# Additions behind the out product of batches 0 and 1, made by adding transfers instead of by VectorE

## The chip, the cores and the metric

The kernel runs on one core of one Trainium2 chip. A core has a matrix engine (TensorE; PE in the profile, with its weight loads as PEld), VectorE (DVE), ScalarE (ACT), GpSimd (POOL) and a queue engine, SyncE (SP). Each takes its own instructions strictly in order and waits on semaphores for the others. DMA transfers are issued by SP, by POOL and, in four places at the end, by ACT. The metric is the device time of one execution in microseconds (us); less is better.

## The reference, cut to what matters

All data are float32. B is 8, H is 8, S is 576, D is 64, and C is H x D, 512.

```python
kv  = einsum('bhsd,bhse->bhde', k, v)                 # attention without softmax
out = einsum('bhsd,bhde->bhse', q, kv)
x   = out / sqrt(mean(out*out, -1) + 1e-6) * g_norm   # then (B, S, H*D)

gate = sigmoid(causal_conv(x, conv_w))                # 5 taps along the sequence, per channel
val  = x @ w_val
y    = (gate * val) @ w_out                           # (B, S, 512)
```

## The kernel before, in words

**Order.** No scheduler chooses the order. A long string, `PLAN`, lists 1235 steps, each a function name with small integers, and the main loop calls them in that order. What a step issues stands behind what earlier steps issued on the same engine. Stores and loads go to the SP queue, in the order of their steps. A tile framework adds the semaphore waits, from the tiles and DRAM regions that an instruction reads and writes.

**Stages of a batch b.** `load_half` and `load_q` bring k, v and q; `kv_product` and `kv_copy` make kv; `turn_q` transposes q on VectorE; `raw_pair b c` makes the attention product of chunks c and c-1 (128 tokens each) in two PSUM banks, `raw_tail` that of the last 64 tokens. `square` (ACT) and `sums` (DVE) give the sums of squares; `powers` (POOL, L552) turns them into reciprocal roots; `normalise` (ACT, L571) scales with them and so frees the PSUM banks of the raw product. `turn_blocks` (DVE, L596) transposes 32x32 blocks into `y`, and `move_blocks b a` (L604) moves `y` into the channel-major tile `xT` with four transfers, two from SP and two from POOL. The last 64 tokens go another way: `turn_x b 4` transposes them on TensorE, and `keep_x` evicts them. `halo` (POOL, L611) fills the four tokens that the convolution looks back to. Then `gate_start`, four times `gate_tap`, `gate_end`, and beside them `x_sums` (DVE, L667) and `val_fast` (PE, L682) for x @ w_val. `gated` leaves gate * val in `gv`.

**The out product.** Two batches make a pair i (i = 0 is batches 0 and 1). A pair has four blocks p of 256 tokens, each with two chunks c = 2p and c = 2p+1 of 128 tokens, and a chunk 8 for the tails of both batches (`out_product`, `keep_out`). The blocks are multiplied by a seven-product scheme: `fast_product i p n`, n = 0 to 6, adds into three half banks, a (one PSUM bank) and b, c (halves of another, named cb). `fast_keep i p n` takes results out when they are due:

- n = 0 and n = 2 (ACT copies, L786 and L790) put a into the low and the high half of the first chunk's tile `ot`; n = 1 (ACT, L788) puts c into the high half of the second chunk's tile; n = 6 (ACT, L797) puts a into its low half.
- n = 5 (DVE, L784 by a helper) adds the whole bank cb, 512 columns, to the first chunk; n = 4 (DVE, same line) adds a, 256 columns, to the high half of the second chunk.

`store i c` (L806) then writes a chunk with four SP transfers of 32 rows of 2 KB.

For pair 0 the plan runs `fast_product` from 73.65 us on, beside batch 1's gates and batches 2 to 4's earlier stages. The string around the second and third store (nothing left out between `store 0 1` and `powers 3 0`):

```
store 0 1; load_q 4 1; store 0 3; gate_tap 1 2 1;
normalise 3 1; halo 2; powers 3 0; ... store 0 2; ... normalise 3 0; fast_keep 0 2 0; turn_blocks 3 0
```

and around its last one:

```
move_blocks 4 2; store 0 7; move_blocks 4 0; kv_copy 5 0; move_blocks 4 1; ... move_blocks 4 3;
... powers 4 4; normalise 4 4; ... turn_x 4 4; ... val_fast 4 0 0
```

Of the kernel before, what the change touches and what calls it, by code (L numbers as in the profile page):

```python
# [9 lines left out]
FP32 = mybir.dt.float32  # L10
U32 = mybir.dt.uint32
AF = mybir.ActivationFunctionType
ALU = mybir.AluOpType
AX = mybir.AxisListType

P = 128
# [191 lines left out]
def kernel(  # L208
# [11 lines left out]
    nc = tc.nc  # L220
    B, H, S, D = q.shape
    C = H * D
    HP = H // 2
    NJ = S // P
# [8 lines left out]
    HB = P // TB  # L233
# [7 lines left out]
    FAST_OUT = 0  # L241
    ROOTS = {(0, 2): H + H // 2, (0, 1): 2 * H}
    GATES = 3
    GVS = 3
    assert NJ == 4 and NB == 18
    assert 2 * T == P and NB * TB == S and SV <= 512 and C <= 512 and D == 2 * TB
# [3 lines left out]
    work = ctx.enter_context(tc.tile_pool(name="work", bufs=2))  # L250
# [9 lines left out]
    xTs = [const.tile([P, NK, SX], FP32, name=f"xT{i}") for i in range(2)]  # L260
    gv = const.tile([P, NK, GVS * S], FP32, name="gv")

# [13 lines left out]
    LOW, HIGH = slice(0, C // 2), slice(C // 2, C)  # L276
# [19 lines left out]
    st = {}  # L296
# [100 lines left out]
    for jt in range(NK):  # L397
        cols = slice(jt * P, (jt + 1) * P)
# [214 lines left out]
    def gate_start(b, jt):  # L613
        gate = work.tile([P, S], FP32, tag="gate", bufs=GATES, name=f"gate{b}_{jt}")
        nc.scalar.activation(  # L615
            out=gate[:], in_=xTs[b % 2][:, jt, HALO:SX], func=AF.Copy, scale=cwT[:, K - 1, jt:jt + 1])
        st["gate", b, jt] = gate
# [22 lines left out]
    def keep_val(b, jt, n):  # L640
        first = b % GVS * S + n * SV
        nc.scalar.copy(out=gv[:, jt, first:first + SV], in_=st["val", b, jt, n][:])

    def gated(b, jt):
        both = gv[:, jt, b % GVS * S:(b % GVS + 1) * S]
        nc.vector.tensor_tensor(out=both, in0=both, in1=st["gate", b, jt][:], op=ALU.mult)  # L646
# [39 lines left out]
    def val_keep(b, mj, n):  # L686
        a, b_, c = (st[bank, "val", b, mj][:] if (bank, "val", b, mj) in st else None for bank in "abc")
        to = lambda o, half: gv[:, mj + 2 * o, b % GVS * S + half * SV:b % GVS * S + (half + 1) * SV]
        add = lambda out, one, two: nc.vector.tensor_tensor(out=out, in0=one, in1=two, op=ALU.add)
# [15 lines left out]
    rows_out = out.rearrange("b (t n) c -> b n t c", n=NB)  # L705

    def out_product(i, c):

        po = ps([P, C], f"out{i}_{c}")
        for jt in range(NK):  # L710
            if c < 2 * NJ:
                first = (2 * i + c // NJ) % GVS * S + c % NJ * P
                nc.tensor.matmul(
# [4 lines left out]
            for r in range(2):  # L718
                first = (2 * i + r) % GVS * S + SF
                nc.tensor.matmul(  # L720
# [57 lines left out]
    def fast_keep(i, p, n):  # L778
        a, b, c = (st.get((bank, i, p)) for bank in "abc")
        row = int(n in (1, 4, 6))  # L780
        if ("ot", i, 2 * p + row) not in st:
            st["ot", i, 2 * p + row] = work.tile([P, C], FP32, tag="ot", bufs=3, name=f"ot{i}_{2 * p + row}")
        first, second = (st.get(("ot", i, 2 * p + r)) for r in range(2))
        add = lambda out, one: nc.vector.tensor_tensor(out=out, in0=one, in1=out, op=ALU.add)  # L784
        if n == 0:
            nc.scalar.copy(out=first[:, LOW], in_=a)  # L786
        elif n == 1:
            nc.scalar.copy(out=second[:, HIGH], in_=c)  # L788
        elif n == 2:
            nc.scalar.copy(out=first[:, HIGH], in_=a)  # L790
        elif n == 4:
            add(second[:, HIGH], a)
        elif n == 5:
            add(first[:], st["bc", i, p][:].rearrange("p r c -> p (r c)"))
        else:
            last = (i, p) == (B // 2 - 1, 2 * NV - 1)
            (nc.vector.tensor_copy if last else nc.scalar.copy)(out=second[:, LOW], in_=a)  # L797

    def store_last(i, c, n):
        store(i, c, nc.scalar if n else nc.sync, range(n * HB // 2, (n + 1) * HB // 2))  # L800

    def store(i, c, queue=nc.sync, blocks=range(HB)):
        ot = st["ot", i, c]
        for j in blocks:
            bb, n = divmod(c * HB + j, NJ * HB) if c < 2 * NJ else (j // 2, NJ * HB + j % 2)
            queue.dma_start(out=rows_out[2 * i + bb, n], in_=ot[j * TB:(j + 1) * TB, :])  # L806

    steps = {f.__name__: f for f in (
        load_half, load_q, load_q_rows, stage_weight, narrow_weight, turn_cw, keep_cw, start_warm, warm_up,
        kv_product, kv_copy, turn_q, turn_q_rows, sort_q, raw_whole, raw_pair, raw_tail, square, sums, powers, normalise,  # L810
        turn_x, keep_x, turn_blocks, move_blocks, halo, gate_start, gate_tap, gate_end, val_product, keep_val, gated,
        val_sums, x_sums, val_fast, val_keep, out_product, keep_out, weight_sums, token_sums, fast_product, fast_keep,
        store, store_last)}
    with tc.manual_schedule():
        set_up()
# [33 lines left out]
```

## Time and profile before

| | |
|---|---|
| time, two runs | 305.83 and 306.24 us, median 306.03 |
| span of the profiled execution | 304.6 us |
| TensorE busy, matmuls (modelled ends) | 294.8 us, 97% |
| VectorE busy | 269.2 us, 88% |
| ScalarE busy | 193.7 us, 64% |
| GpSimd busy | 114.9 us, 38% |
| HBM read, written | 39.21 MB, 9.44 MB |

The profile was taken of one execution, and its span runs from the first to the last instruction. A whole execution's time is some 1.4 us more than this span (306.03 against 304.6). A row of a timeline gives start and duration in us, engine, line, operation and tiles, then how long the engine sat idle before it and which engine ended that. The chain of work that ended last is followed back from the last instruction, at each step to what released it.

### The profile page before, as it was taken

How to read it: one execution, taken by the hardware profiler on the slowest of the kernel's cores; microseconds unless marked ns; L12 is line 12 of the kernel's file. 1: busy time of each engine (PE TensorE's matmuls, PEld its weight loads, DVE VectorE, ACT ScalarE, POOL GpSimd, SP SyncE). 2: the span in 40 equal slices, each digit the busy share in tenths (PEclk: the TensorE clock that was granted, in tenths of full speed). 3: DMA queues.
4: the chain of work that ended last, by engine and by line, in shares of the span. 5: the costliest groups of instructions: out<-in, count | busy, mean ns of one | idle time of the engine just before them, and what ended most of it. 6: DMA issues, size and time to landing. Idle time of an engine off the chain costs nothing.

```text
span 304.6 us, 8977 instructions
## 1 busy us (share of the span) xinstructions
PE 294.8 (97%) x3441; PEld 232.4 (76%) x3441; DVE 269.2 (88%) x474; ACT 193.7 (64%) x596; POOL 114.9 (38%) x127
## 2 busy tenths in 40 slices
PE   7899999999999999999999999999999999999993
PEld 7788778877787785777778757787878588888582
DVE  1169999999999999999999999999999999999612
ACT  1569989999768664884586547683787354535220
POOL 3027354406568217364338352345536631000000
PEclk9979999999999999999999999999999999999999
DMA  7999998088569756988689477927411621112423
GB/s 269 343 368 343 272 302 210 4 230 269 154 147 329 231 163 167 269 220 260 173 253 294 111 175 232 326 72 214 114 48 30 169 80 34 36 42 64 103 69 103
DMA packets 32074, 55.53 MB, mean 182 GB/s; under 512 B 6166, under 2 KB 14358, under 8 KB 32032
## 3 DMA queue, kind: packets, MB, share of 16 engines
q1 hardware_dynamic: 29520, 49.76, 55.7%
q0 software_dynamic: 1632, 3.17, 4.1%
q10 hardware_dynamic: 880, 2.03, 1.8%
q8 instruction: 27, 0.44, 0.6%
q14 instruction: 15, 0.12, 0.1%
HBM read 39.21 MB, written 9.44 MB: 160 GB/s over the span
## 4 chain that ended last, share of the span: by engine, by line
PE 89%; DVE 5%; DMA 2%; issue 1%; ACT 1%; DVEq 0%; ACTq 0%; SPq 0%
PE a L774 18%; PE cb L774 14%; PE va L682 13%; PE val L633 11%; PE vc L682 6%; PE kvps L440 6%; PE raw L501 5%; PE out L720 5%; PE vb L682 4%; PE qTps L477 4%; PE raw L512 2%; PE xTps L583 2%; DMA qs<-in_q_dram 2%; DVE gate L621 2%; DVE xs L667 1%
## 5 line engine op out<-in xcount | busy, mean ns | idle before, releaser
L552 POOL TENSOR_TENSOR rt<-ss,mhalf 128x8 f32<-128x8 f32 (+3 forms) x38 | 68.9, 1822 | 101.0 <-DVE ss L544 100.8
L621 DVE SCALAR_TENSOR_TENSOR gate<-xT,cwT,gate 128x576 f32<-128x576 f32 x128 | 101.8, 809 | 1.0
L571 ACT ACTIVATE x<-raw,rt 128x64 f32<-128x64 f32 x252 | 55.8, 351 | 7.2 <-POOL rt L552 4.2
L604 POOL DMA_DIRECT2D xT<-y x48 | 26.4, 557 | 25.5 <-DVE ot L784 14.0
L633 PE MATMUL val<-xT,wval 128*128 128x288 f32 x128 | 33.0, 411 | 0.0
L774 PE MATMUL a<-wsum,sums 128*128 128x256 f32 x128 | 32.4, 382 | 0.0
L628 ACT ACTIVATE gate<-gate 128x576 f32<-128x576 f32 x32 | 22.0, 692 | 11.7 <-DVE gate L621 11.4
L633 PEld LDWEIGHTS val<-xT,wval 128*128 128x128 f32 x128 | 23.5, 190 | 6.5 <-ACT xT L590 0.4
L544 DVE TENSOR_REDUCE ss<-sq 128x8 f32<-128x520 f32 (+1 forms) x40 | 24.7, 627 | 2.9 <-ACT sq L531 2.5
L774 PEld LDWEIGHTS a<-wsum,sums 128*128 128x128 f32 x128 | 24.0, 190 | 4.1 <-issue 0.6
L535 ACT ACTIVATE sq<-raw 128x256 f32<-128x256 f32 (+1 forms) x70 | 22.4, 403 | 7.3 <-PE raw L501 7.1
L682 PE MATMUL va<-xs,vsum 128*128 128x288 f32 x96 | 26.6, 409 | 0.0
L615 ACT ACTIVATE gate<-xT,cwT 128x576 f32<-128x576 f32 x32 | 25.2, 811 | 1.5 <-DVE gv L646 1.3
L646 DVE TENSOR_TENSOR gv<-gv,gate 128x576 f32<-128x576 f32 x32 | 23.6, 750 | 0.9 <-ACT gate L628 0.8
L682 PEld LDWEIGHTS va<-xs,vsum 128*128 128x128 f32 x96 | 18.0, 190 | 5.1 <-ACT x L571 0.4
L611 POOL COPY xT<-xT 128x124 f32<-128x124 f32 x32 | 17.5, 585 | 10.5 <-ACT xT L590 10.5
L501 PEld LDWEIGHTS raw<-kv,qT 64*64 64x64 f32 x1008 | 16.4, 134 | 5.3 <-issue 3.0
L440 PEld LDWEIGHTS kvps<-v,k 64*64 64x64 f32 x1008 | 15.9, 135 | 3.7 <-issue 1.9
L501 PE MATMUL raw<-kv,qT 64*64 64x64 f32 x1008 | 18.7, 221 | 0.0
L440 PE MATMUL kvps<-v,k 64*64 64x64 f32 x1008 | 17.6, 220 | 0.0
L774 PE MATMUL cb<-wsum,sums 128*128 128x256 f32 x64 | 16.9, 386 | 0.1
L774 PE MATMUL cb<-wout,gv 128*128 128x256 f32 x64 | 16.8, 385 | 0.0
(111 smaller groups left out, 542.3 us busy)
## 6 DMA issues: line engine op xcount, KB each, us to landing
qs<-in_q_dram SPq DMA_DIRECT2D x96, 140.0 KB, 4.2
out_dram<-ot SPq DMA_DIRECT2D x140, 64.0 KB, 1.7
k<-in_k_dram SPq DMA_DIRECT2D x14, 576.0 KB, 6.3
v<-in_v_dram SPq DMA_DIRECT2D x12, 576.0 KB, 6.5
xT<-y SPq DMA_DIRECT2D x48, 64.0 KB, 2.7
xT<-y POOLq DMA_DIRECT2D x48, 64.0 KB, 3.3
y<-in_moe_w_val_dram SPq DMA_DIRECT2D x4, 512.0 KB, 11.4
w_wout<-in_moe_w_out_dram SPq DMA_DIRECT2D x4, 512.0 KB, 6.3
```

Source lines behind the costliest of these rows:

```text
L440: nc.tensor.matmul(st["kvps", b][s][r * D:(r + 1) * D, i], st["k", b, i][rows, r, cols], st["v", b, i][rows, r, cols], start=(j == 0), sto ...
L501: nc.tensor.matmul(st["raw", b, c][r][cols, to * D:(to + 1) * D], st["qT", b][rows, hp, first:first + D], kvs[b % 2][rows, hp, :], start=T ...
L544: nc.vector.reduce_sum(out=st["ss", b][:, FIRST[c]:FIRST[c] + n], in_=st["sq", b, c][:, 0:n], axis=AX.X)
L552: nc.gpsimd.tensor_tensor(out=st["rt", b][:, which], in0=st["ss", b][:, which], in1=mhalf[:, which], op=ALU.pow)
L571: nc.scalar.activation(out=x[:, to * D:(to + 1) * D], in_=raw[:, h * D:(h + 1) * D], func=AF.Copy, scale=root[:, to:to + 1])
L604: (nc.sync if i % 2 else nc.gpsimd).dma_start(out=xTs[b % 2][i * TB:(i + 1) * TB, :, first:first + P], in_=y[a * TB:(a + 1) * TB, i])
L615: nc.scalar.activation(out=gate[:], in_=xTs[b % 2][:, jt, HALO:SX], func=AF.Copy, scale=cwT[:, K - 1, jt:jt + 1])
L621: nc.vector.scalar_tensor_tensor(out=gate[:], in0=xTs[b % 2][:, jt, tap * TB:tap * TB + S], scalar=cwT[:, tap, jt:jt + 1], in1=gate[:], op ...
L633: nc.tensor.matmul(val[:], wval[:, kc, jt * P:(jt + 1) * P], xTs[b % 2][:, kc, HALO + n * SV:HALO + (n + 1) * SV], start=(kc == 0), stop=( ...
L646: nc.vector.tensor_tensor(out=both, in0=both, in1=st["gate", b, jt][:], op=ALU.mult)
L682: nc.tensor.matmul(st[bank, "val", b, mj][:], weights_[:, k], tokens()[:, k], start=(n in (0, 1, 3) and k == 0), stop=(k == NK // 2 - 1), ...
L774: nc.tensor.matmul(st[bank, i, p], tokens()[:, k], weights_[:, k], start=(n < 2 and k == 0), stop=(k == NK // 2 - 1), skip_group_check=True)
```

## The change

A tuple `ADDED_OUT = (0,)` names the pairs concerned: pair 0, that is batches 0 and 1, 8 of the 32 additions of L784. For these, `fast_keep` with n = 4 or 5 no longer adds with VectorE. ScalarE copies the PSUM half or bank into a new SBUF tile, `more4` (256 columns, two buffers) or `more5` (512 columns, one buffer). The chunk's plain store writes the incomplete sum; behind it, in the same step, POOL issues one transfer that adds `more` to these rows of the output (`accum_op=ALU.add`). The plan string is the same.

```diff
+    ADDED_OUT = (0,)
...
+        elif n in (4, 5) and i in ADDED_OUT:
+            part, cols = (a, HIGH) if n == 4 else (st["bc", i, p][:].rearrange("p r c -> p (r c)"), slice(0, C))
+            more = work.tile([P, C if n == 5 else C // 2], FP32, tag=f"more{n}", bufs=6 - n, name=f"more{i}_{p}_{n}")
+            nc.scalar.copy(out=more[:], in_=part)
+            st["more", i, 2 * p + row] = more, cols
         elif n == 4:
             add(second[:, HIGH], a)
         elif n == 5:
...
             queue.dma_start(out=rows_out[2 * i + bb, n], in_=ot[j * TB:(j + 1) * TB, :])
+        if ("more", i, c) in st:
+            more, cols = st["more", i, c]
+            bb, n = divmod(c * HB, NJ * HB)
+            nc.gpsimd.dma_start(
+                out=rows_out[2 * i + bb, n:n + HB, :, cols], in_=more[:], accum_op=ALU.add)
```

In the built program each adding transfer waits for five or six semaphores: those of the four plain stores of its chunk, and those of its own earlier transfer slot and of the ScalarE copy where these are not already known to be past. On the POOL queue the eight of them stand as follows (named by the step that issues them):

```
powers 2 4
ADD store 0 0
move_blocks 2 0, 2 2, 2 1, 2 3     (8 transfers; the last one reuses the semaphore of ADD store 0 0)
powers 3 3, 3 2, 3 1
ADD store 0 1
ADD store 0 3
halo 2
powers 3 0
ADD store 0 2
move_blocks 3 1, powers 3 4, move_blocks 3 3, 3 2, 3 0
ADD store 0 4
powers 4 3
ADD store 0 5
powers 4 2
ADD store 0 6
powers 4 1, 4 0
halo 3
move_blocks 4 2
ADD store 0 7
move_blocks 4 0, 4 1, 4 3
powers 4 4
```

The other engines keep their order, but for the eight additions that leave VectorE and the eight copies that join ScalarE.

## The prediction

> **What bounds the kernel now.** I read the busy times and the chain first:
>
> ```profile
> PE 294.8 (97%) x3441; PEld 232.4 (76%) x3441; DVE 269.2 (88%) x474; ACT 193.7 (64%) x596; POOL 114.9 (38%) x127
> ...
> PE 89%; DVE 5%; DMA 2%; issue 1%; ACT 1%; DVEq 0%; ACTq 0%; SPq 0%
> ```
>
> TensorE holds 89% of the chain, VectorE 5%. PE's busy time is modelled, so I asked for stretches of 10 us around the change (columns: busy us of PE, PEld, DVE, ACT and POOL with counts, granted clock, DMA share, GB/s):
>
> ```profile
> 90.00:100.00 10.00, 10.00 (x44) 8.01 (x43) 9.86 (x15) 8.55 (x30) 8.76 (x8) 1.00 0.94 300
> 100.00:110.00 10.00, 9.66 (x190) 7.79 (x189) 9.96 (x19) 6.97 (x27) 0.62 (x1) 1.00 0.74 209
> ```
>
> Both PE and VectorE are full. That PE really streams shows in the chain: four 288-column matmuls take 0.97 us at their fastest, and 44 matmuls in 10 us is that rate. So an easier VectorE gives little, and a stall of TensorE is not made up later. One place in this stretch is tight, in the chain's pieces (start, length):
>
> ```profile
> 106.44 0.27 ACT x L571
> ...
> 106.85 1.34 ACT x L571 x6
> 108.20 0.04 issue
> 108.24 2.16 PE a L774 x8
> ```
>
> This is `normalise 3 0`: when its last piece ends, PE gets a bank and goes on 0.04 us later. From 89.9 to 106.4 the chain stands on VectorE. What feeds `normalise 3 0` besides is `powers 3 0` on POOL (timeline of POOL):
>
> ```profile
> 92.60 3.71 POOL L552 TENSOR_TENSOR rt<-ss,mhalf 128x8 f32<-128x8 f32 x2 [0.94 <-DVE ss L544]
> 96.27 1.97 POOL L611 COPY xT<-xT 128x124 f32<-128x124 f32 x4
> 98.54 2.08 POOL L552 TENSOR_TENSOR rt<-ss,mhalf 128x8 f32<-128x8 f32 x1 [0.30 <-DVE ss L544]
> 113.09 1.16 POOL L604 DMA_DIRECT2D xT<-y  x2 [12.47 <-DVE ot L784]
> ```
>
> It ends at 100.6, 5.8 us ahead of need. And the stores of the changed chunks (timeline of SP; L320 is `load_q 4 1`, the row of eight is `store 0 3` and `store 0 2`):
>
> ```profile
> 94.04 2.07 SPq L806 DMA_DIRECT2D out_dram<-ot  x4
> 96.80 4.60 SPq L320 DMA_DIRECT2D qs<-in_q_dram  x4
> 101.51 4.34 SPq L806 DMA_DIRECT2D out_dram<-ot  x8
> ```
>
> **Part 1, eight additions leave VectorE.** From the groups by form, 4 of 680 ns and 4 of 408 ns, 4.35 us busy; by the starts of their neighbours they hold 0.60 and about 0.31 us each, 3.6 us of queue time. Worth: only the one at 91.23 lies in the VectorE piece of the chain, 0.6 us at most. Before and after it TensorE streams anyway.
>
> **Part 2, eight copies join ScalarE.** By its copies of PSUM: 128x512 takes 600 ns (L728), 128x256 some 390 ns (L786), so 4 x 0.60 + 4 x 0.39 = 4.0 us on an engine 64% busy. One of them waits: the copy of n = 5 of block 1 needs products that PE ends at 91.02, and behind it stand the squares of batch 3, which ran from 89.9 to 91.28. They now end near 92.9, so `sums 3 2` starts at 92.9, not at 91.83: VectorE's piece is 1.1 us later, and `normalise 3 0` could start at 107.5, not 106.44. At 79 the same pattern (copy behind 79.72, `normalise 2 0` 1.05 us later) is used up by 83.97, where ScalarE sat idle for 1.29 us. Part 1's gain is gone with this; part 3 covers the rest.
>
> **Part 3, eight adding transfers join POOL.** Each waits there for its chunk's stores to land, with the roots and halos queued behind it. Issue: the nearest rows are POOL's own transfers, 557 ns (L604) and 610 ns (L406); I take 0.6. I bound it by 0.5 and, for twice the rows of such a transfer, 1.2.
>
> - `ADD store 0 0`: its plain store no longer waits for VectorE (SP waited 5.8 us for that, until 80.71), so it lands near 82. Nothing urgent is behind it but transfers that start at 82.7. No cost.
> - `ADD store 0 1` and `ADD store 0 3`, **the main cost**. The stores of chunk 1, issued from 94.04, landed after 6.5 to 7.2 us, behind four loads of 576 KB (DMA share 0.94): about 101.5. Those of chunk 3 leave SP from 101.51 on, the last at about 103.1, and took 1.9 us more: 105.0, with part 2's shift upstream 105.3. Only then POOL goes on: 0.6 issue, halo 1.97, powers 2.08 (109.95), and `normalise 3 0` starts at 110.0. From its start to PE's next matmul it took 108.24 - 106.44 = 1.8, so PE goes on at 111.8: **+3.6 us**, with part 2's 1.1 inside it. VectorE loses 2.7 there (its next step waits for the same `normalise`), so it gains 0.9 on PE and does not bound next.
> - `ADD store 0 4`, `0 5`, `0 6` between the roots of batch 4. Their stores need no addition any more and come up to 1.2 us sooner; counted on the old clock they land at 120.3, 122.9 and 130.1. So `powers 4 3` ends at 123.0 and `powers 4 2` at 125.7, against needs at 123.86 and 125.72. No cost, 0 to 1 us.
> - `ADD store 0 7`, **the second cost**. Now POOL issues all eight `move_blocks` of batch 4 and the last root in one run, while SP's half is slower:
>
> ```profile
> 141.35 4.39 POOL L604 DMA_DIRECT2D xT<-y  x8 [4.17 <-issue]
> 145.75 1.04 POOL L552 TENSOR_TENSOR rt<-ss,mhalf 128x4 f32<-128x4 f32 x1
> ```
>
> The stores of chunk 7 leave SP from 143.46 to 145.2 and landed after 3.6 to 4.3 us: 149.4, or 148.5 if fewer POOL transfers run beside them, which I take. Then 0.6 issue, six transfers of 0.55, the root 1.04: 153.4, not 146.8. `normalise 4 4` (0.93) ends at 154.4; PE's `turn_x 4 4` stood at 151.89: +2.6. The transfers for `val_fast 4 0 0`, right behind, land in the same time (151.3 + 3.3 to 4.3). ScalarE has 3.2 us of work backed up behind `normalise 4 4`, so `normalise 5 2` comes 4.0 late, 1.4 more than PE; I take 0.4 of it. **+3.0 us**, bounds 1.6 and 4.4.
>
> Moved bytes: 1.5 MB in, and as much read back, on 55.5 MB; most of it outside the full stretch at 90 to 100. Nothing.
>
> **Who waits for an adding transfer to land?** The last transfer of `move_blocks 2 3` (same semaphore), and the copy into `more5` (one buffer). No row shows such a transfer. From below: 64 KB by POOL lands in 3.3 us (transfers xT<-y); from above: a 576 KB load under the full load took 7.8 us. I take 5, nearer the plain loads' 4.1 to 6. The slacks are then enough: issued at 82, wanted by 89; issued at 110.5, its buffer wanted at 120; issued near 125, wanted near 133. So no cost at 5, and none up to 7.
>
> [...]
>
> **Sum.** 0 + 3.6 + 0 + 3.0 = 6.6 us on a span of 304.6: 311.2. With the 1.4 us around it (306.03 - 304.6), 312.6 us; waits priced at nothing above (0 to 1 us each) add more often than they take, so I say **313.0**. Of this kernel about 2%, 6.1 us, can be told from no change, which is 312.15: the forecast lies close to that.
>
> **The rivals.**
>
> - *Forecast: the roots wait on POOL behind the stores.* 310 to 316: 306.0 and the two costs at their low ends (2.6, if chunk 3's stores run 1 us sooner, and 1.6) or at their high ones (3.6 and 4.4, and 1.8 more for three issues of 1.2). Chance 0.58.
> - *The waits are absorbed.* If PE has other banks to go on with, and chunk 3's and 7's stores land 2 us sooner, 306 to 310. For: 5.8 us of spare at `powers 3 0`. Against: 105.0 is 4.4 us past its old end, 100.6. Chance 0.16.
> - *The adding transfers land late.* [...] Past 7 us the last move of batch 2 and with it `x_sums 2 0` (92.46) slip one for one, of which the fixed stall at 108 hides 3.6; past 9 the copies into `more5` hold ScalarE. With 10 us that is 0 and 1 on top of 313, 314; with 14, 3.4 and 5, 321. For: many such transfers follow each other with one buffer. Against: the output's 64 KB stores land in 1.7. Chance 0.22. [...]
> - *Other side: VectorE was the true bound.* If the 269.2 us of VectorE set the end in this stretch, and the modelled PE only looks full, 3.6 us of queue time come off: 306.0 - 3.6 = 302.4. It decides only if POOL is ready before VectorE reaches 105.7, that is if chunk 3's stores land by 100.5. Against: they were issued at 101.5. Chance 0.04.
>
> **Numbers.** Slower by over 2% (above 312.15): six tenths of the forecast's chance (0.35) and all of the third rival (0.22), 0.57. Within 2%: the rest, 0.42; the other side's 302.4 is within it too. Faster by over 2% (below 299.9) would need more than all eight additions are worth: 0.01. The likeliest case alone spans 310 to 316; for 8 in 10 I take 307.5 to 320, which cuts the low end of the second rival and the high end of the third.
>
> **What would show it.** Right: in the waits, POOL's halo or root waiting for a DMA of the output; `normalise 3 0` starting near 110, PE idle some 3 us ahead of block 3's first product; a second gap of PE ahead of `turn_x 4 4`, with the last root of batch 4 some 6 us later than its neighbours. VectorE's additions 24, ScalarE's busy time up by 4 us. Wrong: PE's gaps the same as before and POOL's waits harmless; or ScalarE waiting for the output's transfers (third rival); or store 0 3 leaving SP before 99.

## The result, and the profile after

The changed kernel takes 329.35 us (328.80 and 329.89), against 306.03 before: a ratio of 1.077, 95% interval 1.071 to 1.084. It is slower by 23 us, where 6.6 were forecast. Its profiled execution has a span of 327.0 us, against 304.6.

Busy times and the shares of the chain that ended last, from the page of the changed kernel (a line of the code has a number one higher than before, behind the new branch six higher; L816 is the adding transfer, L795 the copy into `more`):

```profile
PE 300.6 (92%) x3441; PEld 234.3 (72%) x3441; DVE 267.1 (82%) x466; ACT 196.6 (60%) x604; POOL 123.6 (38%) x135
...
PE 63%; DMA 18%; DVE 4%; SPq 4%; POOL 3%; ACT 2%; issue 2%; ACTq 0%; POOLq 0%; DVEq 0%
```

TensorE held 89% of the chain; now it has 63%, and transfers, which had 2%, have 18%. The stretches of 10 us, with the columns as in the prediction:

```profile
90.00:100.00 10.00, 7.08 (x23) 5.48 (x24) 6.92 (x10) 5.07 (x19) 5.83 (x4) 0.83 0.99 297
100.00:110.00 10.00, 10.00 (x99) 7.83 (x101) 8.17 (x16) 7.03 (x24) 3.73 (x6) 1.00 0.72 179
...
140.00:150.00 10.00, 7.12 (x20) 5.31 (x21) 5.36 (x8) 6.11 (x19) 6.02 (x7) 0.66 0.57 130
...
170.00:180.00 10.00, 8.51 (x82) 5.96 (x81) 7.00 (x12) 6.88 (x27) 3.15 (x2) 0.59 0.84 246
```

At 90 to 100, 23 matmuls stand where 44 stood before. And the granted clock, 1.00 in these stretches before, is 0.83, 0.66 and 0.59 in three of them. So time went in two ways, waits and a slow clock. The waits are these rows of TensorE's timeline, all of those between 86 and 180 us with 0.7 us or more of idle time ahead (before, TensorE came to the first of them, `val_fast 2 0 0`, at 90.85 without a wait):

```profile
92.92 2.23 PE L683 MATMUL va<-xT,wval 128*128 128x288 f32 x4 [4.20 <-DMA xT<-y]
112.83 0.47 PE L502 MATMUL raw<-kv,qT 64*64 64x64 f32 x14 [1.29 <-ACT x L572]
132.65 1.24 PE L683 MATMUL va<-xs,vsum 128*128 128x288 f32 x4 [0.96 <-ACT gv L692]
142.88 2.29 PE L683 MATMUL va<-xs,vsum 128*128 128x288 f32 x4 [4.52 <-ACT gv L692]
168.10 0.88 PE L584 MATMUL xTps<-ident,x 128*128 128x128 f32 x2 [2.16 <-ACT x L572]
172.18 2.26 PE L683 MATMUL va<-xT,wval 128*128 128x288 f32 x4 [1.49 <-DVE ot L785]
```

The slow clock stands at and behind the longer ones (windows of the same kernel; the clock is the third number from the end):

```profile
92.90:96.30 3.40, 3.38 (x8) 2.53 (x9) 2.56 (x4) 0.40 (x1) 3.02 (x2) 0.51 1.04 291
140.70:147.50 6.80, 4.62 (x10) 3.33 (x11) 3.95 (x6) 3.61 (x10) 4.00 (x3) 0.50 0.56 145
168.00:178.30 10.30, 8.71 (x79) 6.09 (x80) 7.43 (x11) 7.85 (x31) 3.27 (x2) 0.50 0.84 234
```

Four products of 288 columns take 2.23 us in the first row above, 1.24 in the third. TensorE runs the same 3441 matmuls in the same order in both kernels, so I set each one's start beside its start before. The differences grow at four stops, and between them they stay flat:

| stop | ahead of | waits | slow clock |
|---|---|---|---|
| 1, at 91 us | `val_fast 2 0 0` | 4.4 | 1.7 |
| 2, at 112 us | the product into the bank of `normalise 3 0` | 1.6 | 0 |
| 3, at 131 to 147 us | `val_fast` of batch 3 | 6.1 (6.5, of which 0.4 is made up behind it) | 2.3 |
| 4, at 166 to 178 us | `turn_x 4 4` and `val_fast 4 0 0` | 4.7 | 3.6 |

Together 24.4 us. The spans differ by 22.4 only, since the execution of before also lost some 2 us to a slow clock near its start (clock 0.87 at 10 to 20 us, where the changed kernel has 1.00).

Who made TensorE wait? GpSimd's timeline:

```profile
79.66 1.19 POOL L816 DMA_DIRECT2D out_dram<-more  x1 [0.31 <-issue]
81.14 3.84 POOL L605 DMA_DIRECT2D xT<-y  x7 [0.29 <-issue]
89.91 0.55 POOL L605 DMA_DIRECT2D xT<-y  x1 [4.93 <-DMA out_dram<-more]
...
104.61 1.20 POOL L816 DMA_DIRECT2D out_dram<-more  x1 [8.68 <-DMA out_dram<-ot]
107.47 1.11 POOL L816 DMA_DIRECT2D out_dram<-more  x1 [1.67 <-DMA out_dram<-ot]
108.17 2.00 POOL L612 COPY xT<-xT 128x124 f32<-128x124 f32 x4
110.15 1.66 POOL L553 TENSOR_TENSOR rt<-ss,mhalf 128x8 f32<-128x8 f32 x1
...
161.97 1.17 POOL L816 DMA_DIRECT2D out_dram<-more  x1 [6.58 <-DMA out_dram<-ot]
162.72 3.71 POOL L605 DMA_DIRECT2D xT<-y  x6
166.00 1.50 POOL L553 TENSOR_TENSOR rt<-ss,mhalf 128x4 f32<-128x4 f32 x1
```

The rows at 104.61 and 161.97 are the waits that the forecast is made of, with halo and root behind the first, six moves and the last root of batch 4 behind the second. The row at 89.91 is one that it had priced at nothing: GpSimd's last move of batch 2 waits until the first adding transfer has landed. The list of waits adds them up (total, times, longest):

```profile
POOL out_dram L816 <- DMA out_dram<-ot: 17.8, 4, 8.7
ACT x L572 <- POOL rt L553: 16.7, 10, 7.3
...
ACT more L795 <- DMA out_dram<-more: 6.2, 3, 3.5
```

The last line is the copies' wait for the buffers of `more`. And the list of transfers (KB each, median us from issue to landing) says why:

```profile
out_dram<-more POOLq DMA_DIRECT2D x4, 256.0 KB, 10.1
...
out_dram<-more POOLq DMA_DIRECT2D x4, 128.0 KB, 8.3
```

The eight landed after 7.4 to 14.2 us; 5 was forecast. In the packet records of the first one a mean of 3.8 packets of rows is in flight at a time (3.5 to 4.0 in those issued at 113.24, 143.50 and 161.97), and a packet of 2 KB takes 178 ns in the median, where those of other queues take 84 to 112. So a transfer of 128 rows moves like four strings of 32 rows.

It is not only the adding transfers that are late. SP's moves `xT<-y` that are being issued between 83 and 84 us, in the changed kernel:

```profile
xT<-y SPq DMA_DIRECT2D x1, 64.0 KB, 9.6
```

and in the kernel before, in the same window:

```profile
xT<-y SPq DMA_DIRECT2D x2, 64.0 KB, 3.7
```

These moves are what stop 1 waits for. `val_fast 2 0 0` needs the moves of `move_blocks 2 0`, `2 1` and `2 2`; the last two of SP's leave at 86.6 and 87.3 us, as they did before, when they landed 2.9 and 3.2 us later. Now they land 5.8 and 5.5 us later, at 92.5 and 92.8, and TensorE goes on at 92.92. The move that GpSimd held until 89.91 belongs to `move_blocks 2 3`; it lands at 93.4, when TensorE has already gone on.

### The profile page after: what moved, and what is told of

Its sections match the earlier page's. It is cut to its first block, busy times and chain, and to the rows that moved or that the text cites. A ratio compares the mean times of both kernels' runs of the same rounds, so it can differ in the third digit from the quotient of the medians.

```text
span 327.0 us, 8998 instructions
## 1 busy us (share of the span) xinstructions
PE 300.6 (92%) x3441; PEld 234.3 (72%) x3441; DVE 267.1 (82%) x466; ACT 196.6 (60%) x604; POOL 123.6 (38%) x135
## 2 busy tenths in 40 slices
DMA packets 36298, 57.13 MB, mean 175 GB/s; under 512 B 9366, under 2 KB 18070, under 8 KB 36256
## 3 DMA queue, kind: packets, MB, share of 16 engines
q0 software_dynamic: 5856, 4.77, 7.7%
HBM read 39.21 MB, written 11.01 MB: 154 GB/s over the span
## 4 chain that ended last, share of the span: by engine, by line
PE 63%; DMA 18%; DVE 4%; SPq 4%; POOL 3%; ACT 2%; issue 2%; ACTq 0%; POOLq 0%; DVEq 0%
PE va L683 12%; PE a L775 12%; PE val L634 10%; PE cb L775 9%; DMA out_dram<-more 7%; PE vc L683 6%; DMA qs<-in_q_dram 4%; PE kvps L441 4%; PE out L721 3%; PE raw L502 3%; DMA xT<-y 3%; DMA v<-in_v_dram 3%; PE vb L683 2%; SPq L605 2%; SPq L812 2%
## 5 line engine op out<-in xcount | busy, mean ns | idle before, releaser
L553 POOL TENSOR_TENSOR rt<-ss,mhalf 128x8 f32<-128x8 f32 (+3 forms) x38 | 70.2, 1854 | 86.5 <-DVE ss L545 86.3
L683 PE MATMUL va<-xs,vsum 128*128 128x288 f32 x96 | 28.2, 426 | 5.5 <-ACT gv L692 5.5
L683 PEld LDWEIGHTS va<-xs,vsum 128*128 128x128 f32 x96 | 18.8, 200 | 11.5 <-ACT gv L692 6.3
L502 PEld LDWEIGHTS raw<-kv,qT 64*64 64x64 f32 x1008 | 17.6, 140 | 7.2 <-issue 3.4
L816 POOL DMA_DIRECT2D out_dram<-more x8 | 9.3, 1162 | 32.8 <-DMA out_dram<-ot 17.8
L683 PE MATMUL va<-xT,wval 128*128 128x288 f32 x48 | 15.8, 461 | 6.1 <-DMA xT<-y 4.2
L612 POOL COPY xT<-xT 128x124 f32<-128x124 f32 x32 | 17.4, 582 | 10.6 <-ACT xT L591 10.6
L502 PE MATMUL raw<-kv,qT 64*64 64x64 f32 x1008 | 20.1, 227 | 1.3 <-ACT x L572 1.3
L597 DVE STREAM_TRANSPOSE y<-x 128x512 f32<-128x512 f32 x24 | 16.4, 696 | 4.9 <-ACT x L572 4.9
```

The lines of the kernel that those rows point to most:

```text
L502: nc.tensor.matmul(st["raw", b, c][r][cols, to * D:(to + 1) * D], st["qT", b][rows, hp, first:first + D], kvs[b % 2][rows, hp, :], start=T ...
L553: nc.gpsimd.tensor_tensor(out=st["rt", b][:, which], in0=st["ss", b][:, which], in1=mhalf[:, which], op=ALU.pow)
L683: nc.tensor.matmul(st[bank, "val", b, mj][:], weights_[:, k], tokens()[:, k], start=(n in (0, 1, 3) and k == 0), stop=(k == NK // 2 - 1), ...
```

## The theories

- **W**: GpSimd waits for the plain stores, and roots, halos and moves queue behind it. This is the forecast.
- **F**: each adding transfer, whose output pattern leads with 4, has only about four packets in flight (3.8); it lands late (7.4 to 14.2 us) and holds back other transfers (9.6 us for a move that took 3.7). I took this for few DMA engines, which no run shows, since the packet records do not name the engine.
- **A**: adding in a transfer is slow by itself.
- **C**: after a long wait TensorE's clock is halved for a while (0.50 from 92.95 to 96.36 us, behind the wait of 4.2 us), which adds to what the wait costs.

The kernel before was run again beside the experiments, with medians of 304.4 to 305.2 us. Times below are medians of 4 to 12 executions, and microseconds given for a ratio are the ratio less one, times 305. In experiments 7 to 10 and 12 the lines ahead of the new branch have the numbers of before.

## Experiment 1: the copies without the transfers

```diff
-            nc.gpsimd.dma_start(
-                out=rows_out[2 * i + bb, n:n + HB, :, cols], in_=more[:], accum_op=ALU.add)
+            pass
```

> The copies into more4 and more5 stay, the adding transfers are left out (the output lacks these eight additions). F, A and W alike: no stall is left, 304 to 308. If the copies on ScalarE or the lost order around them cost something by themselves: 309 or more. If VectorE had been the bound: 302 or less.

306.45 us, ratio 1.0047 (1.0009 to 1.0084): 1.4 us slower than before, though VectorE has eight additions fewer. TensorE's timeline of this kernel shows two gaps that before does not have:

```profile
92.97 1.21 PE L683 MATMUL vc<-xs,vsum 128*128 128x288 f32 x4 [0.68 <-DVE xs L668]
131.53 1.24 PE L683 MATMUL va<-xs,vsum 128*128 128x288 f32 x4 [0.66 <-ACT gv L692]
```

All else, 22 us, is the transfers' doing. And what VectorE saves brings nothing: it was not the bound.

## Experiment 2: the same waits, hardly any bytes

Each adding transfer moves 16 of its columns only (the other columns' additions are left out).

```diff
-                out=rows_out[2 * i + bb, n:n + HB, :, cols], in_=more[:], accum_op=ALU.add)
+                out=rows_out[2 * i + bb, n:n + HB, :, cols.start:cols.start + 16], in_=more[:, 0:16], accum_op=ALU.add)
```

> The changed kernel, but each adding transfer adds only 16 of its 256 or 512 columns (the other sums are left out): the same places, waits and number of instructions and rows, a sixteenth to a thirty-second of the bytes. W: POOL's waits for the stores stay and alone cost 6 to 10: 311 to 317. F by bytes: the first stop and the waits for more5 go. [...]

318.84 us, ratio 1.0441 (1.0397 to 1.0484): 13.5 us, somewhat above the 311 to 317 us that W was given. 1.4 us of it are the copies' and 2.4 the slow clock; so W costs more than the 6.6 forecast even with 8 KB a transfer. Its stops on TensorE:

```profile
92.26 1.21 PE L683 MATMUL vc<-xs,vsum 128*128 128x288 f32 x4 [0.68 <-DVE xs L668]
111.14 0.71 PE L502 MATMUL raw<-kv,qT 64*64 64x64 f32 x14 [4.70 <-ACT x L572]
138.67 1.24 PE L683 MATMUL va<-xs,vsum 128*128 128x288 f32 x4 [0.95 <-ACT gv L692]
```

Stop 1 is down to the gap that the copies alone make; the rest of it needs the bytes. Stop 2 is now 5.1 us by the matmuls' starts, since nothing ahead of it has delayed TensorE, and 2.4 us of slow clock follow (0.5 from 110.5 to 117.3). Stop 3 shrinks, slow clock included, from 8.4 to 1.6, stop 4 from 8.3 to 4.8. The bytes are worth the rest, 23.6 less 13.5, some 10 us. GpSimd's timeline ahead of stop 2 (two adding transfers, halo, root):

```profile
101.27 1.20 POOL L816 DMA_DIRECT2D out_dram<-more  x1 [6.06 <-DMA out_dram<-ot]
104.97 1.11 POOL L816 DMA_DIRECT2D out_dram<-more  x1 [2.50 <-DMA out_dram<-ot]
105.67 2.39 POOL L612 COPY xT<-xT 128x124 f32<-128x124 f32 x4
106.63 3.49 POOL L553 TENSOR_TENSOR rt<-ss,mhalf 128x8 f32<-128x8 f32 x1
```

The transfers of this kernel land sooner, but not at once:

```profile
out_dram<-more POOLq DMA_DIRECT2D x8, 8.0 KB, 6.2
```

So the bytes are not all of the landing time. But moves beside them are not held: the medians of `xT<-y` are 2.7 us (SP) and 3.0 (GpSimd), against 3.3 and 3.6 in the changed kernel and 2.7 and 3.3 before.

## Experiment 3: each transfer in four

```diff
-            nc.gpsimd.dma_start(
-                out=rows_out[2 * i + bb, n:n + HB, :, cols], in_=more[:], accum_op=ALU.add)
+            for j in range(HB):
+                nc.gpsimd.dma_start(
+                    out=rows_out[2 * i + bb, n + j, :, cols], in_=more[j * TB:(j + 1) * TB, :], accum_op=ALU.add)
```

The output pattern leads with 32 now. Bytes, packets with rows and places stay; there are 32 instructions instead of 8, and 3072 packets of 8 bytes that the whole transfers have are gone. Experiment 2 has those packets, and its moves are not held; so they are not what makes stop 1.

> Each adding transfer is issued as four, one for each of the chunk's four groups of 32 rows, so that its output pattern leads with 32 and not with 4; same bytes, same waits. [...] Theory A (the adding itself is slow, whatever the engines): landing stays at 7 us or more, time 325 to 340. Theory W (POOL's waits for the stores alone make the loss): 326 to 333.

320.37 us, ratio 1.0512 (1.0439 to 1.0585), below what A (325 to 340) and W (326 to 333) were given: about 8 us of 23 come back. The transfers land in 2.5 to 8.0 us, median 3.6, with up to 23 packets in flight:

```profile
out_dram<-more POOLq DMA_DIRECT2D x16, 64.0 KB, 3.5
...
out_dram<-more POOLq DMA_DIRECT2D x16, 32.0 KB, 5.1
```

Of stop 1 0.9 us is left, and stop 2 has grown to 5.4 us. The time is within 2.5 us of experiment 2, which hardly moved bytes. So, spread out like this, the bytes cost little and W is left.

## Experiment 4: the same transfers without adding

`accum_op` is left out, so the output's rows are overwritten and the additions missing.

```diff
-                out=rows_out[2 * i + bb, n:n + HB, :, cols], in_=more[:], accum_op=ALU.add)
+                out=rows_out[2 * i + bb, n:n + HB, :, cols], in_=more[:])
```

> The same transfers, in the same places with the same waits and the same pattern, but they write more over the output and do not add (the eight additions are left out). [...] A: they land in 2 to 4 us like other transfers of 128 to 256 KB, time 309 to 316. W: time unchanged, 326 to 333.

323.9 us, ratio 1.0570 (1.0485 to 1.0656): 17.4 of the 23.6 us remain. Adding accounts for some 6 us, and the transfers land after 4.5 to 9.3 us, median 6.2, instead of 9.8; A is a part and not the cause.

## Experiment 5: three buffers for the wide copies

```diff
-            more = work.tile([P, C if n == 5 else C // 2], FP32, tag=f"more{n}", bufs=6 - n, name=f"more{i}_{p}_{n}")
+            more = work.tile([P, C if n == 5 else C // 2], FP32, tag=f"more{n}", bufs=n - 2, name=f"more{i}_{p}_{n}")
```

> more5 gets three buffers instead of one, nothing else is changed. If ScalarE's waits for the landed transfer (6.2 us in three waits) are what PE loses at its third stop (8.9 us there with the slow clock): time 319 to 324. If POOL's late roots would hold the same spot anyway: 327 to 331.

327.12 us, ratio 1.0677 (1.0588 to 1.0765). The largest piece of stop 3, 4.7 us at 131 to 143, falls to 1.1: there ScalarE had waited 3.47 us for the buffer, and `gv` behind it. But stop 1 is 1.4 us longer, two gaps just ahead of 131 are 1.5 longer together, and two of 1.2 and 1.3 us are new behind it. Of what one stop loses the others take up nearly all.

## Experiment 6: TensorE kept busy in two of the stops

Small matmuls into a bank that the next product overwrites: 100 ahead of `val_fast 2 0 0`, 60 each ahead of `turn_x 4 4` and `val_fast 4 0 0`.

```diff
+    FILL = {("val_fast", 2, 0, 0): 100, ("turn_x", 4, 4): 60, ("val_fast", 4, 0, 0): 60}
...
+        for _ in range(n):
+            nc.tensor.matmul(to, ident[:, 0:TB], ident[:, 0:TB], start=True, stop=True, skip_group_check=True)
```

> The changed kernel with 100 small matmuls (32x32, overwritten by the next product) ahead of val_fast 2 0 0 and 60 each ahead of turn_x 4 4 and val_fast 4 0 0, so that TensorE works through part of its stalls. Theory C (a stall of TensorE is followed by 3.4 us or more at half the granted clock, which adds 1.7 us at the first stop and 3.6 at the last): granted clock 1.00 there, time 323 to 327. If the clock falls whatever TensorE does, or the small matmuls only delay: 329 to 333.

335.66 us, ratio 1.0979 (1.0904 to 1.1054): slower still. But the clock, windows of this kernel:

```profile
90.00:100.00 10.00, 9.93 (x191) 8.97 (x188) 3.87 (x6) 4.34 (x15) 5.47 (x4) 1.00 0.96 271
...
110.00:120.00 10.00, 6.55 (x169) 5.55 (x169) 9.13 (x17) 4.13 (x16) 5.26 (x7) 0.76 0.70 166
...
170.00:180.00 10.00, 9.18 (x241) 8.35 (x241) 7.42 (x11) 5.96 (x21) 3.93 (x3) 1.00 0.75 206
```

is 1.00 where the fillers stand (stops 1 and 4) and low where none does (stop 2). So TensorE keeps its clock where it is kept busy, as C has it. The fillers took longer than the waits that they stood in (stop 1: 7.05 us of them), so no time came of it; shorter ones were not tried.

## Experiments 7 and 8: the transfers later on GpSimd, split and whole

Three buffers, and a step `add_out` of its own: chunk 0's behind `move_blocks 2 3`, those of 1, 3, 2 behind `store 0 2` (past `powers 3 0`), 4, 5, 6 behind `halo 3`, 7 behind `powers 4 4`. Experiment 7 has the transfers in four, experiment 8 whole.

```diff
-move_blocks 2 3; raw_pair 3 3;
+move_blocks 2 3; add_out 0 0; raw_pair 3 3;
...
-gated 1 3; store 0 2; val_fast 2 1 3;
+gated 1 3; store 0 2; add_out 0 1; add_out 0 3; add_out 0 2; val_fast 2 1 3;
...
-powers 4 0; halo 3; val_fast 3 1 5;
+powers 4 0; halo 3; add_out 0 4; add_out 0 5; add_out 0 6; val_fast 3 1 5;
...
-powers 4 4; normalise 4 4;
+powers 4 4; add_out 0 7; normalise 4 4;
```

> The adding transfers are split in four as in e1_split, more5 has three buffers, and all of them stand later on POOL: chunk 0 behind the moves of batch 2, chunks 1, 3 and 2 behind powers 3 0, chunks 4 to 6 behind halo 3, chunk 7 behind powers 4 4. Theory W+F (waits on POOL and too few engines together are the whole loss): no stall of PE over 2 us, 305 to 309, near the 306.45 of the kernel without the transfers. If extra traffic or issues on POOL matter by themselves: 310 to 316.

> As e5_late_split, but each adding transfer is one instruction again (output pattern leading with 4). W without F: 306 to 309, the same as e5_late_split. [...]

Split: 312.25 us, ratio 1.0227 (1.0178 to 1.0277). Whole: 323.55 us (320.70 to 327.52), ratio 1.0601 (1.0498 to 1.0705). At the same places the whole transfers cost 11 us more by the medians, and still 8 to 9 by the two shortest of their four executions. Both times are above what W+F and W without F were given, 305 to 309 and 306 to 309; the split one lies in the 310 to 316 that were given if the traffic or the issues matter by themselves. The split version has one stop left, 3.6 us at 149 and 1.4 us of slow clock: twelve issues behind `halo 3` push the moves of batch 4 and `powers 4 4` back (the moves start at 146.1 us, before at 141.4; 1.2 of the 4.7 is older lateness).

## Experiments 9 and 10: in GpSimd's idle places, split and whole

The trace of before shows GpSimd idle for 8.0 us behind `powers 4 2`, 4.8 behind `powers 4 4` and 5.8 behind `powers 5 3`.

```diff
-powers 4 2; normalise 4 2;
+powers 4 2; add_out 0 4; add_out 0 5; normalise 4 2;
...
-halo 3; add_out 0 4; add_out 0 5; add_out 0 6; val_fast 3 1 5;
+halo 3; val_fast 3 1 5;
...
-powers 4 4; add_out 0 7; normalise 4 4;
+powers 4 4; add_out 0 6; normalise 4 4;
...
-powers 5 2; powers 5 3; load_half v 6 1;
+powers 5 2; powers 5 3; add_out 0 7; load_half v 6 1;
```

> As the version with later, split adding transfers (312.25 us, 7.1 above before), but the last four chunks' transfers stand where GpSimd sits idle in the trace of before: chunks 4 and 5 behind powers 4 2 (idle for 8 us), chunk 6 behind powers 4 4 (idle for 4.7 us), chunk 7 behind powers 5 3 (idle for 5.7 us). Theory W (what the change costs is work of GpSimd queued behind the adding transfers): the stop of TensorE at 148.8 us (3.6 us and 1.4 us of half clock) goes, and 306.5 to 308 us are left, the copies' 1.4 us among them. Theory F (it is the transfers' traffic on the DMA engines that costs): as many bytes and packets as before, so 311 to 313 us.

> As the version with split adding transfers in GpSimd's idle places (307.34 us, 2.5 above before), but each chunk's adding transfer is again one instruction whose output pattern leads with 4. If the place on the GpSimd queue is all that matters, 306 to 308 us as with the split ones, since POOL issues 8 instructions instead of 32. [...]

Split: 307.34 us, ratio 1.0082 (1.0050 to 1.0113), 2.5 us above before. W is right: the same bytes, packets and instructions as in experiment 3, now with three buffers for the wide copies, cost next to nothing there. GpSimd's timeline of this kernel shows a place taken up without delay to what follows (the moves were at 141.35 and the last root at 145.75 before):

```profile
123.91 6.38 POOL L817 DMA_DIRECT2D out_dram<-more  x8
132.06 3.87 POOL L552 TENSOR_TENSOR rt<-ss,mhalf 128x8 f32<-128x8 f32 x2 [1.78 <-DVE ss L544]
135.89 1.04 POOL L611 COPY xT<-xT 128x124 f32<-128x124 f32 x4
141.15 4.44 POOL L604 DMA_DIRECT2D xT<-y  x8 [4.22 <-issue]
145.61 1.62 POOL L552 TENSOR_TENSOR rt<-ss,mhalf 128x4 f32<-128x4 f32 x1
```

Whole, at the same places: 324.5 us, ratio 1.0606 (1.0525 to 1.0686), far above the 306 to 308 expected if the place is all that matters. So place alone does not help either; F is right too. The first stop shows how. The first adding transfer stands behind all of batch 2's moves on GpSimd, but SP issues its last move at the same time. Transfers issued between 88.2 and 89.3 us, whole:

```profile
out_dram<-more POOLq DMA_DIRECT2D x1, 256.0 KB, 10.5
xT<-y SPq DMA_DIRECT2D x1, 64.0 KB, 8.1
```

and at the same step, 87 to 88.2 us, split:

```profile
out_dram<-more POOLq DMA_DIRECT2D x4, 64.0 KB, 3.6
xT<-y SPq DMA_DIRECT2D x1, 64.0 KB, 4.0
```

The late move was issued from 88.1 us on and landed 8.1 us later, at 96.25; `x_sums 2 0`, which reads what it brings, starts at 96.38, and at 92.18 in the split version. TensorE waits for that; its timeline of the whole version has

```profile
97.28 1.21 PE L682 MATMUL vc<-xs,vsum 128*128 128x288 f32 x4 [3.67 <-DVE xs L667]
...
169.51 2.26 PE L682 MATMUL va<-xT,wval 128*128 128x288 f32 x4 [4.63 <-DMA out_dram<-more]
```

The second row, `val_fast 4 0 0`, is the same again. It waits for several transfers, and the row names the adding one; the last that it needs is a move of SP that was issued at 160.9 and landed 8.5 us later, at 169.4.

## Experiments 11 and 12: the copy of block 1 behind the squares

On ScalarE the copy of n = 5 of block 1 now stands behind the squares that it had delayed.

```diff
-fast_keep 0 1 5; square 3 0; fast_product 0 1 6; square 3 2; sums 3 2;
+square 3 0; square 3 2; fast_keep 0 1 5; fast_product 0 1 6; sums 3 2;
```

Experiment 11 makes this edit in experiment 1's kernel, which leaves the eight additions out; experiment 12 in experiment 9's.

> The copies alone, without adding transfers (8 additions left out; 306.45 us, 1.4 above before), with the copy of n = 5 of block 1 behind the squares 3 0 and 3 2 on ScalarE instead of ahead of them. If that copy's place costs the 1.4 us (the prediction's part 2: sums 3 2 starts 1.1 us late), 305.0 to 305.6 us. If the copies cost because ScalarE as a whole has less room, 306.2 to 306.7 us. If VectorE bounds something once the copies' place is mended, below 304.5 us.

> Both edits together: the adding transfers split and in GpSimd's idle places, and the copy of block 1 behind the squares. If the two costs are separate, the time is that of the first less what the second wins, 305.5 to 307 us: not faster than before. If VectorE's eight additions were worth anything on the path, below 304.5 us. If the traffic costs wherever it stands, 311 us or more.

Copies alone: 305.52 us, ratio 1.0023 (0.9994 to 1.0053), not told apart from before. The gap at 93 us is gone, the one at 131 stays. With the transfers split and in the idle places: 305.79 us, ratio 1.0046 (1.0019 to 1.0073). This is the best form of the change that was run, and still not faster than before.

## Why the prediction was wrong, by its steps

- **What bounds the kernel, and part 1 (VectorE's relief, 0.6 us at most): right as far as the runs show.** With nearly every other cost mended the eight additions win nothing (1.0023 and 1.0046). The gap of 0.7 us at 131 is still there in both, so a gain of that size may be hidden.
- **Part 2 (copies, +1.1 us at `sums 3 2`): right in place, the size nearly.** `sums 3 2` is late and `x_sums 2 0` behind it, so the price shows ahead of `val_fast` at 93 us (0.7 us), not at `normalise 3 0`. A second 0.7 us, at 131, was not foreseen.
- **`ADD store 0 1` and `0 3` (+3.6 us): mechanism right, size low.** Where nothing else delays TensorE (experiment 2) it is 5.1 us. The missing 1.5 us are spread over the sum (1.3 us added to that kernel's times, for the old clock). Chunk 3's last store lands at 105.7 and not 105.3; the forecast lets it leave SP at 103.1, which is the third of its four in the trace of before, and the fourth leaves at 103.53. From that landing to the halo it is 1.3 us, where 0.6 was taken for the issue. Halo and root take 4.45 us together, where 4.05 was taken. The issue of `ADD store 0 1` costs nothing: GpSimd sits idle for 2.50 us behind it. The upper bound of an issue, 1.2 us, is met, but its reason, twice the rows, is not what the runs show: without adding as many rows take 0.76 (experiment 4).
- **`ADD store 0 7` (+3.0 us): the first part is right to 0.3 us.** With the 13.8 us by which all was late there taken off, GpSimd's wait ends at 148.2 (forecast 148.5), the last root at 153.7 (153.4), and `turn_x 4 4` is 2.6 late (2.6). Wrong is what I let follow: 0.4 us more, where `val_fast 4 0 0` waits another 2.1. GpSimd's moves for it, beside the adding transfer, land 7.5 us after their issue, where 3.3 to 4.3 were taken, and an addition of VectorE that it also waits for ends 0.3 us later still.
- **"I take 5 ... So no cost at 5, and none up to 7": the step that failed most.** The transfers land after 7.4 to 14.2 us. The users that were named (the last move of batch 2, the copies into the buffers of `more`) did wait: 4.9 us on GpSimd, 6.2 on ScalarE. TensorE did not stand for the first of these; the longest on ScalarE, 3.47 us, stands ahead of the largest piece of stop 3. The rows that the 5 was taken from, plain loads and moves, have patterns that lead with 32 or 128 and not with 4; in pieces that lead with 32 the same bytes land after 2.5 to 8.0 us (experiment 3). The third rival, which adds up landings at 10 and at 14 us, was the sounder half of the text, at a chance of 0.22. No run of before shows its 14 us; the whole transfers took up to 14.2. Bytes alone do not make the time: with 8 KB the transfers still take 6.2 us in the median (experiment 2).
- **"Moved bytes ... Nothing": wrong in kind.** As bytes they are next to nothing (experiment 9, 1.0082). No page shows the reading back that was counted there: HBM read is 39.21 MB before and after, and what the transfers move rises from 55.53 to 57.13 MB. But while a whole transfer runs as four strings for 8 to 10 us, transfers of other queues are held: 9.6 us for a move that took 3.7. What holds them was not shown, since the packet records do not name the engine. The trace shows that all moves issued beside the first adding transfer but one land only after it has, at 89.6 us, one close behind the other, and that they are not held where the same bytes go in four pieces (4.0 us for a move of experiment 9, 8.1 in experiment 10). The sum had no term for this and neither had the third rival, which therefore stopped at 321. Stop 1, 6.1 us, is for the most part this and the slow clock behind it: it is down to 0.9 us where the transfers are split, and where they carry hardly any bytes.
- **`ADD store 0 4` to `0 6` (0 to 1 us): about right as priced.** In experiment 2 stop 3 is 1.6 us, 0.7 of it the copies'. That it is 8.4 us in the changed kernel goes with the bytes; its largest piece, 4.7 us, is the wait for a buffer of a transfer that has not landed (experiment 5).
- **The slow clock: no term at all.** 7.6 us in the changed kernel, 2.4 behind the one long wait of experiment 2. Each of my waits was priced as if TensorE went on at its old rate.

Of 24.4 us of stops 7.6 are the slow clock, and experiments 2 and 3 put 8 to 10 (slow clock included) on bytes that go through a pattern that leads with 4. The forecast's 6.6 are its two waits alone at full clock; experiment 2 has 5.1 and 4.8 for them. The two causes overlap. Mending the pattern alone leaves 15.6 us, the place alone 18.5, both 2.5 (the last two with three buffers as well): at each stop several things come late together, and taking one away uncovers the next. What stays open is how the 6 us of experiment 4 divide between the longer issue (1.16 against 0.76 us) and the later landing (9.8 against 6.2 us in the median).

## What to carry to other kernels

Before handing work to a transfer, look in a trace at how many packets of one of its pattern are in flight (here 3.8 for a whole transfer, up to 23 with the transfers in four), and ask which other queue's transfers run during that time (here 9.6 us for a move that took 3.7); the bytes alone do not say what it will hold up. An instruction that waits on an in-order queue belongs where that queue is idle in the trace, with all that it issues counted. Where TensorE is the bound, a wait (here of 2.2 to 4.5 us) can have a second price behind it, the slow clock (0.50).

## What the hardware showed that I had not expected

- A wait of TensorE can halve its clock, for 3.4, 6.8 or 10.2 us. The waits of 4.2, 4.5 and 2.2 us in the changed kernel were followed by 0.50, and one of 1.3 us was not; but in experiment 10 one of 3.67 us was not either (clock 1.00 from 97.4 to 101), where one of 2.17 us was. So the length of the wait alone does not decide it. Where the wait lies goes a long way. In the changed kernel the slow stretches begin at 92.95, 140.74 and 168.04 us, 14 and 8 times 3.413 us apart, and last one, two and three times that; in experiment 10 they begin at 119.35, 133.00 and 167.14, 4 and 10 times that apart. Pieces of that length, laid out from these starts, cut the wait of 3.67 us at 95.46 into 1.85 and 1.82, while that experiment's wait of 2.17 ahead of 118.05 lies in one piece but for 0.06. In the changed kernel the pieces at full clock with 3.38, 2.37 and 2.10 us of idle TensorE came just before 0.50, and none with 1.42 or less, up to its last matmul, did. It is not the whole rule: before, where the kernel starts up, the piece from 13.93 to 17.34, with 1.69 us of idle time, came before 0.50 too.
- An adding transfer is dear: 1.16 us of GpSimd to issue one of 128 rows (0.76 without adding), 178 ns for a packet of 2 KB in the median, and, in the whole transfers, three packets of 8 bytes more for each row. The packets of GpSimd's queue rose from 1632 to 5856, of which only 1024 are rows of `more`; with the transfers split it is 3168.
- Four strings of packets were enough to make 64 KB moves of SP and of GpSimd, those issued from 80 to 85 us, take 7.4 to 9.6 us instead of 2.5 to 3.8, at a mean DMA share of 0.54 (80 to 90 us; 0.50 before).
